# Fused decayed linear attention and dense layer: other order of the first loads, of the first groups' steps and of the third group's transposes

## The chip, the cores and the metric

The kernel runs on one core of one Trainium2 chip. The metric is the device time of one execution in microseconds (us). A core has five engines that work beside each other, each with a queue of its own in program order: TensorE (PE, matrix products; PEld is its loading of weights), VectorE (DVE), ScalarE (ACT), GpSimd (POOL) and SyncE (SP). POOL issues all loads that turn float32 into float16, SP issues the outputs and the transposes that the DMA engines make.

## The reference

Two parts in a row. First an attention without softmax, with a decay per head, worked block by block with a running state; then a dense layer with the Mish activation, `h * tanh(softplus(h))`.

```python
# q, k, v: (4, 8, 768, 64); lam: (8,)
for b in range(nb):                       # blocks of the sequence
    intra = einsum('bhic,bhjc->bhij', qb, kb) * Dmask      # lam ** (i - j) for i >= j
    intra = einsum('bhij,bhjd->bhid', intra, vb)
    inter = einsum('bhid,bhde->bhie', qb * lam_pow, kv_state)
    out[:, :, sl] = intra + inter
    kv_state = lam_block * kv_state + einsum('bhsd,bhse->bhde', kb * rev_pow, vb)
# dense layer: x (3072, 512), w_in (512, 2048), w_out (2048, 512)
h = x @ w_in
g = h * tanh(log1p(exp(h)))
return g @ w_out
```

## The kernel before

**Groups and chunks.** The sequence of 768 is cut into six groups `n` = 0 to 5 of 128 positions; each has four chunks `b` = 0 to 3, one for each of the four batches, of 128 positions and 8 heads. Chunks come in two pairs: 0 and 1 (lower), 2 and 3 (upper). A chunk's attention is: *turn* (k and q transposed, `turn_pe` on PE or `turn_dma` by DMA for a pair), *scores* (`raw_scores`: kT times qT), *masks* (`masked`, DVE, two products with the decay table `dm` to `sb`), `kd` (`decay_k`: k times its decay), *state* (product of `kd` and v, then `raw` and the new state `w`), *outputs* (`outputs`: q times state plus `sb` times v in PSUM bank z, then DVE makes `xn`). `xn` is turned to `xt` by PE (`back`) or by a DMA transpose. Group 0 has no state yet and goes through `first_outputs`.

**Dense layer.** A *unit* (`unit`, token `u`) is 128 of the 2048 hidden columns for the 512 rows of a group: four matmuls of 512 columns from `xt` and a quarter of w_in (`win[0]` to `win[3]`, four units each), then Mish on ACT into `hsg`. `two_units` does two of them for half the rows; `unit_part` does a piece of columns of a unit. Groups 4 and 5 use a seven-product scheme (`set_step`, tokens `m1` to `m7`). The second layer is `dense2_plain` (group 0, tokens `plain`) and `dense2` (groups 1 to 4, tokens `h`, with seven products), and `dense2_alone` for group 5 at the end.

**What sets the order.** Everything is written out by hand: `run(d, order, banks)` takes a string of tokens, and each token issues the instructions of one step on all its engines at that place. `s:0@0` is the scores of chunk 0 of group 0; without `@` an attention step belongs to the group after `d`. Each engine works through its own instructions in just this order. Semaphores hold back what is not ready. `fill:m` issues `m` products of zeros on PE (bank H). `k:b` puts `kd` on DVE, `k:b/p` on POOL; `st:b/tag/v` or `/p` puts the last product of the state on DVE or POOL. `load:k/1@2` is the load of k's upper pair of group 2, at POOL's turn. In the order of names below `win_71` to `win_74` are `win[0]` to `win[3]`, and `wout_75` to `wout_78` the four quarters of w_out; `vz` is v of group 0 with zeros between its heads.

**The start.** k and q of chunk 0 come as float32 through SP and ACT (`whole`) and are turned to float16 by ACT (`k0`) and DVE (`q0`). All other loads go through POOL, in the order in which they are written. The decay tables `dm` are made by DVE (`d:0`, `d:1`, four instructions each) and ACT (`e:0`, `e:1`, exponentials). `mish` loads ACT's table for the Mish function.

**Buffers.** k, q and v of later groups have four pair buffers each, so the load of a pair waits until the steps of an earlier pair that read its buffer are done.

Of the kernel before, what the change touches and what calls it, by code (L numbers as in the profile page):

```python
# [20 lines left out]
def kernel(  # L21
# [10 lines left out]
    nc = tc.nc  # L32
# [32 lines left out]

    def bank(tag, shape, dtype=F32):
        return ps.tile([128] + shape, dtype, name=f"b{tag}", tag=f"b{tag}")
# [49 lines left out]
    def load_wout(s):  # L117
# [13 lines left out]

    load_first("k", 0, queue=nc.sync)
# [5 lines left out]
    load_first("q", 1)  # L138
    load_first("v", 0, 2)
    load_first("k", 2, 2)  # L140
    nc.gpsimd.iota(ek, pattern=[[0, 1]], base=MID, channel_multiplier=-1,
                   allow_small_or_imprecise_dtypes=True)
    nc.gpsimd.iota(eq, pattern=[[0, 1]], base=-MID, channel_multiplier=1,
                   allow_small_or_imprecise_dtypes=True)
# [12 lines left out]

# [16 lines left out]
    def busy(m):  # L174

        t = bank("H", [4 * C])
        for _ in range(m):
            nc.tensor.matmul(t, kzero, kzero2, start=True, stop=True)

    def fill(m):  # L180

        t = bank("H", [C])
        for _ in range(m):
            nc.tensor.matmul(t, kzero, kzero, start=True, stop=True)
# [59 lines left out]
    def turn_pe(n, b, banks):  # L244
# [6 lines left out]
        for src, name, to, tag in zip(srcs, ("kT", "qT"), (kT, qT), banks):  # L251
            pt = bank(tag, [JP, C], F16)
# [27 lines left out]
    def raw_scores(n, b, tags):  # L280
        p_ = [bank(t, [JP, C]) for t in tags]
# [18 lines left out]
    def first_outputs(b, tag):  # L300
        po = bank(tag, [JP, C])
# [9 lines left out]
    def outputs(n, b, turn=None):  # L311

        done.add(("o", n, b))
        po = bank("z", [H, D])
        for j in range(JP):
# [15 lines left out]
        def later():  # L331
            pt = bank(turn, [JP, C], F16)
# [8 lines left out]
    def state(n, b, tag, eng, later=False):  # L341
        need("o" if n else "lbm", n, b if n else 0)
        done.add(("st", n, b))
        pv = bank(tag, [JP, 128])
# [24 lines left out]
    open_ = {}  # L369

    def unit_part(n, ni, tag, lo, hi, opens):
        need("x", n, range(lo // C, hi // C))
        if (n, ni) not in open_:
            open_[n, ni] = bank(tag, [GT])
        for kc in range(NKC):
# [5 lines left out]
    def unit_end(n, ni):  # L381
        nc.scalar.activation(h_tile(n)[:, ni, :], open_.pop((n, ni)), AF.Mish)  # L382
        done.update(have("g", n, ni, range(2)))

    def unit(n, ni, tag):
        unit_part(n, ni, tag, 0, GT, True)
# [9 lines left out]
    def two_units(n, ni, r):  # L396

        t = bank(next_bank(), [2, HC])
        cs = slice(r * HC, r * HC + HC)
# [79 lines left out]
    def set_step(o, step):  # L479
# [4 lines left out]
        if step == "m1":  # L484
            o.a = bank(o.banks[0], [2, HC])
            seven(o, 1, o.a, True)
        elif step == "seed":
            o.b = bank(o.banks[1], [2, HC])
            nc.scalar.activation(o.b, o.a, AF.Copy)
# [3 lines left out]
        elif step == "m5":  # L493
            o.c = bank(o.banks[2], [2, HC])
            seven(o, 5, o.c, True)
# [114 lines left out]
    def dense2(n):  # L610
# [3 lines left out]
        def half(p, blk):  # L614
            if blk == 0 and p in (1, 5, 3):
                m.g = bank("G", [2, HN])
            t = m.g if p in (1, 2, 5, 3) else m.h
# [3 lines left out]
            if p == 1:  # L621
                m.h = bank("H", [2, HN])
                nc.scalar.activation(m.h, m.g, AF.Copy)
# [24 lines left out]
    def dense2_plain(n, b, part, tag):  # L648

        if part == 0:  # L650
            open_[n, "out"] = bank(tag, [DMO])
        need("wout", part)
        po = open_[n, "out"]
        for kk in range(NKI // WS):
# [3 lines left out]
                             start=(ki == 0), stop=(ki == NKI - 1))  # L658
        if part == WS - 1:
# [58 lines left out]
    def run(d, order, banks=""):  # L718

        sets = [set_of(d, int(b[0]), b[1:]) for b in banks.split()]  # L720
        for token in order.split():
# [9 lines left out]
            elif op == "part":  # L731
                lo, hi = int(tags[1][0]) * C, int(tags[1][1]) * C
                unit_part(d, int(arg), tags[0], lo, hi, lo == 0)
# [136 lines left out]
```

## Time and profile before

| what | value |
|---|---|
| time, median of 3 runs | 204.89 us (204.76 to 205.01) |
| the profiled execution: time, span | 205.89 us, 204.1 us |
| mean granted clock of TensorE | 1.000 |
| busy: PE, PEld, DVE, ACT, POOL | 196.3, 147.1, 144.7, 96.1, 71.4 us |
| loads by POOL's queue | 13.37 MB |
| by the queues of SP and ACT | 12.26 MB and 0.33 MB |

The span runs from the first to the last instruction of the core; some 1.8 us of the time lie around it. An engine's busy time is the time in which at least one of its instructions runs. A row of the timeline has the start in us, the duration, the engine, the line, the operation and its tiles (output, then inputs), and in brackets the idle time before it and what ended that. PE's matmuls overlap, so the step from one start to the next tells more than the durations. A landing time runs from the start of the issuing instruction to the last byte.

### The profile page before, as it was taken

To read this page: it belongs to the slowest core of one execution; us is meant where nothing else is said; L and a number is where in the kernel's file an instruction comes from. 1 tells how busy PE (TensorE), PEld (TensorE's weight loads), DVE (VectorE), ACT (ScalarE), POOL (GpSimd) and SP (SyncE) were. 2 spreads that over 40 slices of the span, in tenths; PEclk is the share of its full clock that TensorE was granted. 3 is DMA by queue.
4 is the path that set the end of the run, shared out by engine and by line. 5 is a ranking of instruction groups with operands and counts; after the bars stand their busy time and mean duration, and the time that the engine had idled before them with its cause. 6 is when DMAs were issued, how large, how long until landed. Compare 5 with 4: busy or idle time off the path is not lost.

```text
span 204.1 us, 4535 instructions
## 1 busy us (share of the span) xinstructions
PE 196.3 (96%) x1879; PEld 147.1 (72%) x1879; DVE 144.7 (71%) x241; ACT 96.1 (47%) x170; POOL 71.4 (35%) x68
## 2 busy tenths in 40 slices
PE   7897999799999999999999999999999999999993
PEld 3675556588875556677576766868888988888893
DVE  6638558867784999379699795986949795097333
ACT  4554676757641124331534444145673474864310
POOL 7987454533254395047113377070000000000020
PEclk9999999999999999999999999999999999999999
DMA  8999999999969999999999399999210621002223
GB/s 128 130 166 206 165 181 157 172 206 190 139 128 115 206 171 177 126 182 151 115 203 162 79 80 130 127 285 130 79 29 22 115 71 55 2 0 72 85 76 129
DMA packets 109302, 26.24 MB, mean 129 GB/s; under 512 B 99426, under 2 KB 108770, under 8 KB 109282
## 3 DMA queue, kind: packets, MB, share of 16 engines
q0 software_dynamic: 77536, 13.37, 93.1%
q1 hardware_dynamic: 30560, 12.26, 31.7%
q10 hardware_dynamic: 1186, 0.33, 0.7%
q8 instruction: 14, 0.23, 0.5%
q14 instruction: 6, 0.05, 0.1%
HBM read 27.26 MB, written 6.29 MB: 164 GB/s over the span
## 4 chain that ended last, share of the span: by engine, by line
PE 89%; ACT 3%; DMA 3%; POOL 1%; DVE 1%; issue 1%; POOLq 0%
PE bG L604 15%; PE bH L604 13%; PE bA L376 7%; PE bB L376 7%; PE bC L376 6%; PE bB L471 3%; DMA vz<-in_v_dram 3%; PE bC L471 3%; PE bA L471 3%; PE bB L404 3%; PE bz L316 2%; PE bz L321 2%; PE bA L404 2%; PE bC L404 2%; PE be L285 2%; PE bA L657 2%
## 5 line engine op out<-in xcount | busy, mean ns | idle before, releaser
L356 POOL TENSOR_TENSOR w<-raw,lbm 128x512 f16<-128x512 f32 x14 | 21.1, 1509 | 54.9 <-DVE raw L354 54.9
L604 PEld LDWEIGHTS <-gsum 128*128 128x128 f16 x336 | 31.1, 98 | 4.6
L376 PEld LDWEIGHTS <-win 128*128 128x128 f16 x200 | 18.3, 98 | 16.3 <-issue 1.0
L604 PEld LDWEIGHTS <-hsg 128*128 128x128 f16 x240 | 23.2, 98 | 4.2
L324 DVE TENSOR_TENSOR xn<-bz,lq 128x512 f16<-128x512 f32 x20 | 13.8, 688 | 11.7 <-PE bz L321 11.6
L688 POOL TENSOR_TENSOR c<-p,u 128x512 f32<-128x512 f32 x1 | 1.3, 1260 | 58.3 <-DVE p L687 58.3
L604 PE MATMUL bH<-tsum,gsum 128*128 128x256 f16 x160 | 20.3, 273 | 0.0
L604 PE MATMUL bG<-wout,hsg 128*128 128x256 f16 x160 | 20.1, 273 | 0.0
L376 PE MATMUL bA<-xt,win 128*128 128x512 f16 (+2 forms) x72 | 17.6, 367 | 0.6 <-ACT xt L308 0.6
L295 DVE TENSOR_TENSOR sb<-be,dm 128x512 f16<-128x512 f32 x17 | 11.6, 684 | 8.4 <-PE bo L285 8.4
L278 DVE TENSOR_TENSOR kd<-kn,lk 128x512 f16<-128x512 f16 x20 | 16.6, 848 | 0.0
L376 PE MATMUL bB<-xt,win 128*128 128x512 f16 (+2 forms) x68 | 16.6, 367 | 0.0
L376 PE MATMUL bC<-xt,win 128*128 128x512 f16 x60 | 15.4, 379 | 0.0
L382 ACT ACTIVATE hsg<-bB 128x512 f16<-128x512 f32 x16 | 9.6, 598 | 12.1 <-PE bB L376 12.1
L382 ACT ACTIVATE hsg<-bA 128x512 f16<-128x512 f32 x17 | 10.2, 597 | 9.5 <-PE bA L376 9.5
L382 ACT ACTIVATE hsg<-bC 128x512 f16<-128x512 f32 x15 | 9.0, 599 | 10.1 <-PE bC L376 10.0
L471 PEld LDWEIGHTS <-wsum 128*128 128x128 f16 x128 | 12.5, 98 | 1.5
L559 DVE TENSOR_TENSOR gsum<-hsg 128x1024 f16<-128x1024 f16 x20 | 13.5, 680 | 0.0
L404 PEld LDWEIGHTS <-win 128*128 128x128 f16 x128 | 12.1, 98 | 1.8
L104 POOL DMA_DIRECT2D kn<-in_k_dram x10 | 11.8, 1179 | 2.9 <-PE bo L346 1.4
L104 POOL DMA_DIRECT2D vn<-in_v_dram x10 | 11.7, 1173 | 2.8 <-DMA win<-in_moe_w_in_dram 2.0
L104 POOL DMA_DIRECT2D qn<-in_q_dram x10 | 11.6, 1156 | 2.2 <-PE bA L376 0.9
(164 smaller groups left out, 406.0 us busy)
## 6 DMA issues: line engine op xcount, KB each, us to landing
out_dram<-osum SPq DMA_DIRECT2D x23, 256.0 KB, 2.4
kn<-in_k_dram POOLq DMA_DIRECT2D x11, 256.0 KB, 10.7
qn<-in_q_dram POOLq DMA_DIRECT2D x11, 256.0 KB, 12.7
vn<-in_v_dram POOLq DMA_DIRECT2D x10, 256.0 KB, 10.2
wout<-in_moe_w_out_dram POOLq DMA_DIRECT2D x4, 512.0 KB, 15.1
win<-in_moe_w_in_dram POOLq DMA_DIRECT2D x3, 512.0 KB, 12.2
vz<-in_v_dram POOLq DMA_DIRECT2D x2, 256.0 KB, 7.1
k<-in_k_dram SPq DMA_DIRECT2D x1, 256.0 KB, 3.3
```

The source lines that it names most:

```text
L104: nc.gpsimd.dma_start(out=tile_, in_=rows(src, n, 2 * bp, 2))
L278: eng.tensor_tensor(out=kd[n, b], in0=kn[n, b], in1=bc(lk, 2, D), op=ALU.mult)
L285: nc.tensor.matmul(p_[t][:, j, :], kT[n, b][rs, j, :], qT[n, b][rs, j, :], start=True, stop=True)
L295: nc.vector.tensor_tensor(out=sb[n, b, t], in0=p_[t], in1=dm[:, t], op=ALU.mult)
L324: nc.vector.tensor_tensor(out=xn, in0=po, in1=bc(lq, 2, D), op=ALU.mult)
L356: decay = lambda: eng.tensor_tensor(out=w_new, in0=raw, in1=lbm, op=ALU.mult)
L376: nc.tensor.matmul(open_[n, ni][:, lo:hi], win[ni // 4][:, kc, (ni % 4) * 128 : (ni % 4) * 128 + 128], xt[n][:, kc, lo:hi], start=(opens a ...
L382: nc.scalar.activation(h_tile(n)[:, ni, :], open_.pop((n, ni)), AF.Mish)
L404: nc.tensor.matmul(t[:, u, :], win[ni // 4][:, kc, m : m + 128], xt[n][:, kc, cs], start=(u == 0 and kc == 0), stop=(kc == NKC - 1), skip_ ...
L471: nc.tensor.matmul(t[:, u, :], lhs, rhs, start=(fresh and u == 0 and kk == 0), stop=(kk == 1), skip_group_check=True)
L559: nc.vector.tensor_tensor(out=gsum[n, i][:, ks, :], in0=a, in1=b, op=op)
L604: nc.tensor.matmul(t, lhs(kk, blk), rhs(kk)[:, lo:hi], start=(fresh and kk == 0), stop=(kk == HK - 1), skip_group_check=True)
```

## The change

- **First loads.** q and k of the upper pair of group 0, and its v, come as single chunks. The upper half of `win[0]` (columns 256 to 512) is loaded right behind the second chunk's k, its lower half far later and in one piece instead of two. `ek` and `eq` (`iotas`) are made later. v of group 1's lower pair comes behind `win[3]`.
- **Order of steps.** All six groups' token strings are reordered; the first three most. In group 0, `q0` stands ahead of the decay tables on DVE, the exponentials behind the first turn on ACT, and `mish` behind the third output. The first whole unit is 10 and not 2. Zero products: 64 in smaller pieces instead of 38.
- **kd on POOL.** Seven of the `kd` products move from DVE to POOL (`k:3/p@1`, `k:1/p`, `k:2/p`, `k:3/p` while group 1's units run, and `k:0/p`, `k:1/p`, `k:3/p` later).
- **Third group.** Loads of k for a pair need that the turn of the same pair two groups earlier was issued; `turn` and `load` tokens stand further apart.
- **Helpers.** `unit_part` and `dense2_plain` may take their parts in any order (the first one opens the bank); `pieces` and `parts` only keep account of banks and parts while the kernel is written out, and issue nothing.

POOL's queue from its first load on (`kn`, `qn`: k and q; 128x8x64 is one chunk, 128x16x64 a pair; `win_71` at 128x4x128 is a quarter of `win[0]`). Before:

```order
L94 DMA kn<-in_k_dram 128x8x64
L136 ISA
L136 IOTA rel 128x128
L94 DMA qn<-in_q_dram 128x8x64
L94 DMA vz_69<-in_v_dram 128x16x64
L94 DMA kn<-in_k_dram 128x16x64
L141 IOTA ek 128x1
L143 IOTA eq 128x1
L94 DMA qn<-in_q_dram 128x16x64
L94 DMA vz_70<-in_v_dram 128x16x64
L113 DMA win_71<-in_moe_w_in_dram 128x4x128 x2
L113 DMA win_71<-in_moe_w_in_dram 128x4x256
```

With the change, from the iota on:

```order
L146 IOTA rel 128x128
L117 DMA win_71<-in_moe_w_in_dram 128x4x256
L96 DMA qn<-in_q_dram 128x8x64
L96 DMA vz_69<-in_v_dram 128x16x64
L96 DMA qn<-in_q_dram 128x8x64
L96 DMA kn<-in_k_dram 128x8x64 x2
L96 DMA vz_70<-in_v_dram 128x8x64
L96 DMA qn<-in_q_dram 128x8x64
L137 IOTA ek 128x1
L139 IOTA eq 128x1
L117 DMA win_71<-in_moe_w_in_dram 128x4x256
L96 DMA vz_70<-in_v_dram 128x8x64
```

Half of `win[0]` moved ahead of the second chunk's q; the upper pair's q, k, k, v, q stand singly behind the first v, and the last v behind the other half of `win[0]`.

PE where the last pieces of units 0 and 1 end and the first whole unit starts. Before (`win_71` is `win[0]`, so unit 2):

```order
L376 MATMUL bB<-xt,win_71 128x128
L376 LDWEIGHTS win_71
L376 MATMUL bB<-xt,win_71 128x128
L376 LDWEIGHTS win_71
L376 MATMUL bC<-xt,win_71 128x512
```

With the change (`win_73` is `win[2]`, so unit 10):

```order
L394 MATMUL bB<-xt,win_71 128x128
L394 LDWEIGHTS win_71
L394 MATMUL bB<-xt,win_71 128x128
L394 LDWEIGHTS win_73
L394 MATMUL bC<-xt,win_73 128x512
```

The first unit reads another quarter of w_in, whose load stands two places further on in POOL's queue.

ACT around the turn of chunk 2 of group 1, while group 0's last units run (`hsg` are Mish activations, `xt<-bG` the copy of a turned-back output, `kT<-bH` and `qT<-bz` the copies of a turn). Before:

```order
L382 ACTIVATE hsg<-bB 128x512
L336 ACTIVATE xt<-bG 128x4x128
L260 ACTIVATE kT<-bH 128x512
L260 ACTIVATE qT<-bz 128x512
L382 ACTIVATE hsg<-bC 128x512
L336 ACTIVATE xt<-bG 128x4x128
```

With the change:

```order
L401 ACTIVATE hsg<-bB 128x512
L269 ACTIVATE kT<-bH 128x512
L269 ACTIVATE qT<-bz 128x512
L349 ACTIVATE xt<-bG 128x4x128
L401 ACTIVATE hsg<-bC 128x512
L401 ACTIVATE hsg<-bA 128x512
L349 ACTIVATE xt<-bG 128x4x128
```

The copies of the turn stand ahead of the copy of the first output, which came first.

The diff, cut (of each table of tokens the beginning):

```diff
@@ load_pair
             for i in (2 * bp, 2 * bp + 1):
                 need({"k": "kd", "q": "turn", "v": "o"}[t], n - 2, i)
+                if t == "k":
+                    need("turn", n - 2, i)
...
@@ first loads
     load_first("k", 1)
     nc.gpsimd.iota(rel, pattern=[[1, C]], base=0, channel_multiplier=-1,
                    allow_small_or_imprecise_dtypes=True)
-    load_first("q", 1)
-    load_first("v", 0, 2)
-    load_first("k", 2, 2)
...
-    load_first("q", 2, 2)
-    load_first("v", 2, 2)
-    load_win(0, 0, 128)
-    load_win(0, 128, 256)
-    load_win(0, 256, WQ)
-    load_win(2)
-    load_win(1)
-    for t in "kqv":
-        load_pair(t, 1, 0)
-    load_win(3)
-    for t in "kqv":
-        load_pair(t, 1, 1)
+    def run_loads(order):
+        for token in order.split():
+            t, *args = token.split("/")
+            args = [int(x) for x in args]
...
+    run_loads("""
+        w/0/256/512 q0/1 v0/0/2 q0/2 k0/2 k0/3 v0/2 q0/3 iotas w/0/0/256 v0/3 w/2 w/1 k/1/0 q/1/0
+        w/3 v/1/0 k/1/1 q/1/1 v/1/1""")
@@ group 0's attention
-        k0 d:0 q0 e:0 d:1 fill:6 pe:0/Gz@0 e:1 fill:6 s:0@0 mask pe:1/Gz@0 heads fill:4 first:0/C
...
+        k0 q0 fill:4 d:0 d:1 fill:3 pe:0/Gz@0 fill:3 fill:5 s:0@0 e:1 fill:3 fill:4 e:0 pe:1/Gz@0
+        fill:3 fill:7 s:1/AB@0 mask heads first:0/C mask fill:1 fill:3 pe:2/Gz@0 first:1/C s:2@0
...
@@ group 0's units
-        u:2 u:3 st:0/e/v@0 k:2@0 u:8 st:1/o/v@0 k:3@0 load:k/0@2 load:q/0@2 load:v/0@2 wout:0
...
+        u:10 wout:0 u:9 load:q/1@2 load:k/0@2 u:11 u:2 st:0/e/v@0 k:2@0 st:1/o/v@0 load:q/0@2
...
@@ unit_part
-        if (n, ni) not in open_:
+        opens = (n, ni) not in open_
+        if opens:
             open_[n, ni] = bank(tag, [GT])
@@ dense2_plain
-                             start=(ki == 0), stop=(ki == NKI - 1))
-        if part == WS - 1:
+                             start=(not made and kk == 0), stop=(kk == NKI // WS - 1),
+                             skip_group_check=True)
+        made.append(part)
+        if len(made) == WS:
```

More of the change, by code (lines that the diff above doesn't have):

```diff
@@ L64, in need @@
         assert not missing, missing
+    pieces = set()
     def bank(tag, shape, dtype=F32):
@@ L182, in fill @@
         t = bank("H", [C])
+        pieces.add("H")
         for _ in range(m):
@@ L331, in later @@
         def later():
+            pieces.add(turn)
             pt = bank(turn, [JP, C], F16)
@@ L381, in unit_end @@
     def unit_end(n, ni):
+        need("part", n, ni, range(4))
         nc.scalar.activation(h_tile(n)[:, ni, :], open_.pop((n, ni)), AF.Mish)
@@ L488, in set_step @@
             o.b = bank(o.banks[1], [2, HC])
+            assert o.banks[1] not in pieces
             nc.scalar.activation(o.b, o.a, AF.Copy)
@@ L622, in half @@
                 m.h = bank("H", [2, HN])
+                assert "H" not in pieces
                 nc.scalar.activation(m.h, m.g, AF.Copy)
@@ L648, in dense2_plain @@
     def dense2_plain(n, b, part, tag):
-        if part == 0:
-            open_[n, "out"] = bank(tag, [DMO])
+        if (n, b) not in parts:
+            parts[n, b] = (bank(tag, [DMO]), [])
+            pieces.discard(tag)
+        po, made = parts[n, b]
         need("wout", part)
-        po = open_[n, "out"]
         for kk in range(NKI // WS):
@@ L802 @@
+        fill:4 mask pe:3/Gz@0 fill:1 fill:1 k:1@0 fill:8 first:2/C s:3@0 states mish fill:6
+        part:0/A/03 fill:2 mask fill:2 fill:1 first:3/C k:0@0 fill:1 fill:2 part:1/B/03
+        part:0/A/34 part:1/B/34 end:0 end:1""")
     run(0, """
-        u:2 u:3 st:0/e/v@0 k:2@0 u:8 st:1/o/v@0 k:3@0 load:k/0@2 load:q/0@2 load:v/0@2 wout:0
-        wout:1 wout:2 wout:3 load:k/1@2 load:q/1@2 load:v/1@2 u:9 st:2/e/v@0 u:10 st:3/o/v@0 masks
-        u:11 u:4 u:5 pe:0/Hz k:0 u:6 u:7 s:0 mask pe:1/Hz k:1 u:12 o:0 st:0/H/v/l s:1 mask decay:0
@@ L806 @@
-        u:13 back:0 pe:2/Hz k:2 u:14 o:1 st:1/H/v/l s:2 mask decay:1 back:1 pe:3/Hz u:15""")
+        u:10 wout:0 u:9 load:q/1@2 load:k/0@2 u:11 u:2 st:0/e/v@0 k:2@0 st:1/o/v@0 load:q/0@2
+        k:3@0 k:1 u:5 u:3 masks u:7 pe:0/Hz u:6 wout:2 st:3/o/v@0 st:2/e/v@0 wout:3 pe:1/Hz
+        load:v/0@2 u:13 s:0 k:0 wout:1 mask u:12 u:8 load:k/1@2 o:0 u:4 s:1 pe:2/Hz back:0 u:14
+        mask st:0/H/v/l o:1 u:15 st:1/H/v/l back:1 s:2 load:v/1@2 pe:3/Hz decay:1 k:2 decay:0 mask""")
     run(1, """
-        k:3@1 two:0/0 two:2/0 o:2@1 st:2/H/p@1 s:3@1 mask two:4/0 two:6/0 back:2@1 o:3@1
@@ L815 @@
-        busy:1 h h""")
+        two:4/0 two:2/0 two:6/0 o:2@1 k:3/p@1 load:k/0@3 s:3@1 two:0/0 two:8/0 mask back:2@1 o:3@1
+        k:1/p two:10/0 st:3/H/v@1 back:3@1 two:12/0 pe:0/Hz two:4/1 turn:1 two:0/1 st:2/H/p@1
+        two:14/0 s:0 mask pe:1/HG k:0 two:6/1 two:14/1 o:0 st:0/H/v s:1 two:2/1 plain:0/1 two:10/1
+        mask o:1 q:0/0 q:0/1 st:1/H/p load:v/0@3 two:12/1 load:q/0@3 q:1/01 k:2/p plain:0/0
+        two:8/1 plain:1/1 plain:1/2 plain:2/1 s:2 mask plain:1/0 plain:0/2 s:3 o:2 turn:0@3 mask
```

77 lines of the change are left out of this document (47 added, 30 removed).

## The prediction

> **What bounds the kernel now.** I read the page's busy line first, then the stretches, the waits of PE and the timeline.
>
> ```profile
> PE 196.3 (96%) x1879; PEld 147.1 (72%) x1879; DVE 144.7 (71%) x241; ACT 96.1 (47%) x170; POOL 71.4 (35%) x68
> ```
> ```profile
> 0.00:20.70 20.70, 17.24 (x159) 12.33 (x160) 12.65 (x31) 10.84 (x20) 17.33 (x24) 1.00 1.60 158
> ...
> 32.00:40.00 8.00, 6.87 (x86) 4.45 (x85) 7.15 (x12) 4.97 (x11) 3.62 (x4) 1.00 2.42 162
> 40.00:190.00 150.00, 150.00 (x1442) 114.47 (x1441) 114.44 (x180) 70.16 (x124) 43.13 (x34) 1.00 1.18 123
> 190.00:204.10 14.10, 10.87 (x116) 9.76 (x113) 4.10 (x10) 1.79 (x3) 1.26 (x1) 1.00 0.27 93
> ```
>
> In the stretches (length, then PE, PEld, DVE, ACT and POOL busy, granted clock, DMA share, GB/s) PE never stops between 40 and 190 us. Nothing that the change does to loads, transposes or DVE there can gain; it can only cost. The last stretch (3.23 us idle) runs the same final part. What can be gained lies in two places: the start, up to the first whole unit of the dense layer, and 8.00 - 6.87 = 1.13 us of idle PE between 32 and 40.
>
> ```profile
> 20.70 1.03 PE L376 MATMUL bC<-xt,win 128*128 128x512 f16 x4
> 21.56 1.03 PE L376 MATMUL bA<-xt,win 128*128 128x512 f16 x4
> ...
> 22.65 1.03 PE L376 MATMUL bB<-xt,win 128*128 128x512 f16 x4
> ```
> ```profile
> PE bz L316 <- ACT qT L260: 0.6, 1, 0.6
> ...
> PE bG L334 <- DVE xn L324: 0.2, 1, 0.2
> PE bH L254 <- DVE raw L354: 0.2, 1, 0.2
> ```
>
> Up to 20.70 PE has made the first group's attention and units 0 and 1; there unit 2 starts (a unit is four matmuls, 0.86 from start to start), at 22.65 unit 8, the first on w_in's third quarter. The changed order has the same work ahead of that point, and then unit 10. So the first term is when that point comes; zero products ahead of it count as busy, but are no work.
>
> **The first stretch.** What the loads can give:
>
> ```profile
> 6.00:7.00 1.00, 0.90 (x9) 0.90 (x10) 1.00 (x5) 0.74 (x2) 1.00 (x3) 1.00 0.96 61
> ...
> 9.00:10.00 1.00, 0.48 (x6) 0.22 (x5) 0.70 (x2) 0.65 (x4) 1.00 (x3) 1.00 2.41 154
> 16.00:17.00 1.00, 0.50 (x12) 0.32 (x8) 0.49 (x1) 0.62 (x2) 1.00 (x2) 1.00 1.34 207
> ```
> ```profile
> 3.50 1.15 POOL L94 DMA_DIRECT2D vz<-in_v_dram  x1
> ...
> 5.94 1.19 POOL L94 DMA_DIRECT2D qn<-in_q_dram  x1
> ...
> 8.25 3.73 POOL L113 DMA_DIRECT2D win<-in_moe_w_in_dram  x5
> ```
> ```profile
> vz<-in_v_dram POOLq DMA_DIRECT2D x1, 256.0 KB, 6.4
> ```
> ```profile
> qn<-in_q_dram POOLq DMA_DIRECT2D x1, 256.0 KB, 7.3
> ```
> ```profile
> win<-in_moe_w_in_dram POOLq DMA_DIRECT2D x1, 512.0 KB, 10.4
> ```
>
> q, k and v pass at 154 KB/us, w_in at 207, and between 6 and 7 the engines ran nearly dry (61): the first v had been issued at 3.50 and its data was not yet there. It landed at 9.9. The change puts 256 KB of w_in (1.24 us) into that hole. POOL's issues move by one w_in issue (3.73 / 5 = 0.75), so v of the first pair moves by 0.75: I take its landing at 10.65. Behind it come five single chunks of 128 KB, 128/154 = 0.83 each: q2 11.5, k2 12.3, k3 13.1, v2 14.0, q3 14.8; then w_in's lower half 16.0, v3 16.9. In all, ahead of the end of w2 (the third quarter, units 8 to 11) the same bytes pass as before, less the hole. Before, w2 was the fourth of the five w_in issues (about 10.5) and landed at 10.5 + 10.4 = 20.9; with 0.5 to 0.7 us of the hole filled: 20.2 to 20.4. The other end: if the time from issue counted, not the bytes ahead, w2 (issued at about 12.25, behind more issues) would land at 22.65. Adding 512/207 to v3's 16.9 would even give 19.4. I take 20.3, since the queue is busy from 7 us on and the bytes ahead of w2 decide, and keep both far ends.
>
> The Trainium skill (page "DMA: Bandwidth & Descriptors", section "Anatomy of one DMA — SWDGE (gpsimd) path") gives each such DMA a fixed cost of about 2.0 us beside its bytes, and speaks against splitting loads. By it three more DMAs would be an estimated 6 us, 210 in the end, if the fixed part were not hidden. The rows differ: from 9 to 10 the data moves at 154 KB/us without a gap while q of the upper pair, issued at 5.94, takes 7.3 to land, with k and v in flight beside it: the fixed part overlaps.
>
> Now the engines, with the durations of these rows:
>
> ```profile
> 3.62 1.01 DVE L201 SCALAR_TENSOR_TENSOR dm<-rel,lnb,gone 128x128 f32<-128x128 f32 x4
> ...
> 4.66 0.63 ACT L793 ACTIVATE dm<-dm 128x512 f32<-128x512 f32 x1
> ...
> 5.36 0.68 DVE L795 CAST qn<-q 128x512 f16<-128x512 f32 x1 [0.73 <-DMA q<-in_q_dram]
> ...
> 8.08 0.69 DVE L295 TENSOR_TENSOR sb<-be,dm 128x512 f16<-128x512 f32 x1 [1.00 <-PE bo L285]
> ...
> 11.53 1.03 PE L184 MATMUL bH<-kzero 128*128 128x128 f16 x8
> ...
> 13.64 1.28 ACT L790 ACT_TABLE_LOAD   x1
> ...
> 15.56 0.61 PE L184 MATMUL bH<-kzero 128*128 128x128 f16 x8
> ```
>
> DVE now casts q first, and so stands until 5.36; the two decay tables follow at 6.04 to 8.1 (2 x 1.01) instead of one at 3.62, their exponentials on ACT at 8.15 to 9.4. The first two masks therefore run at about 10.1 to 11.4, against 8.08 before. The first output (which before waited for v at 9.9) starts at 11.4, with v there since 10.65: a late table costs 0.75 beyond the load. From there each step hangs on the one before: masks of chunk 1 to 12.7; turns of chunk 2 (k2 at 12.3) at 12.85; its scores 14.35, masks to 16.05; third output 16.4; its copy on ACT 17.1 to 17.7. The table load (1.28) now stands behind that copy and not ahead of the second one: 17.7 to 19.0. DVE puts one kd and the lbm copies ahead of the last masks, which end at 18.65. Fourth output 18.8, its copy 19.3 to 19.9; the remaining pieces of units 0 and 1 end at 20.55. That is 0.15 ahead of 20.70. The 26 further zero products (64 against 38) lie in these waits: at 0.08 to 0.13 each (0.61 / 8, 1.03 / 8) 2 to 3 us of PE that would be idle. If the waits around them shrank, those right ahead of the pieces (11, 0.9 us) would cost. Term one: -0.15, with ends of -0.7 (tables not late, since DVE's order alone sets that) and +1.95 (w2 at 22.65).
>
> **32 to 40 us.**
>
> ```profile
> 18.22 1.17 POOL L104 DMA_DIRECT2D qn<-in_q_dram  x1
> ```
> ```profile
> qn<-in_q_dram POOLq DMA_DIRECT2D x1, 256.0 KB, 16.4
> ```
> ```profile
> 35.09 0.39 PE L254 MATMUL bz<-ident,qn 128*128 128x128 f16 x4
> ...
> 35.34 0.59 ACT L336 ACTIVATE xt<-bG 128x512 f16<-128x512 f16 x1
> ...
> 36.29 0.62 ACT L260 ACTIVATE qT<-bz 128x512 f16<-128x512 f16 x1
> ...
> 36.96 0.38 PE L316 MATMUL bz<-w,qT 128*128 128x128 f16 x4 [0.62 <-ACT qT L260]
> ```
>
> The turn of chunk 2 ends on PE at 35.31 (its last four transposes, of 128 columns each, take a quarter of a unit's 0.86); the outputs of chunk 1 need bank z, which ACT empties (qT) only at 36.9, because the copy of xt ran first (0.59). Between them stood one unit (0.86). Now the turn-back (0.23), the unit and a state product (0.23) stand between, 1.32, and ACT copies kT and qT ahead of xt: z is free some 1.1 after the turn. The 0.62 goes. The second turn-back waited 0.23 for xn: 0.57 of PE work (a state product, one scores) stood between, now a unit and a state product, 1.1: gone. The wait for raw (0.19) keeps its distance (scores and turn-back change places) and stays. What is late next is q of the upper pair of group 1, which landed at 18.22 + 16.4 = 34.6 and, with the hole filled, would at 34.2, while its turn now stands at 20.55 + 13.4 = 33.95 by the durations of the steps between: a wait of 0.2. w3 lands at about 29.2 for unit 13 at 29.35. Term two: -0.62 - 0.23 + 0.2 = -0.65, with ends of -0.85 (q in time) and -0.2 (q at 34.6).
>
> **From 40 us on.** Seven kd products move from DVE to POOL.
>
> ```profile
> 40.61 0.68 DVE L278 TENSOR_TENSOR kd<-kn,lk 128x512 f16<-128x512 f16 x1
> ...
> 46.95 2.36 DVE L278 TENSOR_TENSOR kd<-kn,lk 128x512 f16<-128x512 f16 x2
> ...
> 47.12 1.65 POOL L356 TENSOR_TENSOR w<-raw,lbm 128x512 f16<-128x512 f32 x1 [1.81 <-DVE raw L354]
> ```
>
> The Trainium skill (page "GPSIMD Engine Reference", section "Engine selection") calls two-input work there about 2 times slower and says that it shares interfaces with VectorE. The rows agree: DVE's two kd took 2.36 while POOL's 1.65 ran, against 2 x 0.68 alone. So DVE gains nothing for sure, 7 x 0.68 less against up to 7 x 1.0 more; with 35.6 of 150 us idle it covers both. POOL's own queue: kd stands behind loads that wait for earlier loads, but each kd is used 4 us or more later. Without that cover one late kd would cost PE a microsecond.
>
> Group 3's transposes, a k load that ran alone (issued at 59.92), and the landing of the first transpose:
>
> ```profile
> kn<-in_k_dram POOLq DMA_DIRECT2D x1, 256.0 KB, 4.7
> ```
> ```profile
> kT<-kn SPq DMA_TRANSPOSE x1, 9.3
> ```
> ```profile
> 80.03 4.09 SPq L268 DMA_TRANSPOSE qT<-qn  x1
> ```
>
> Beside queued loads one issue took 4.09 and one landing 9.3, and PE was full all the same. Holding POOL's loads back shortens these, which is worth 0. But group 4's k load of the lower pair now stands on POOL behind the state product of group 3's chunk 1: near 89, where its scores stand at about 107 (both by adding the durations of the steps). Load 4.7, one issue 4.09 and a landing of 9.3 make 18.1 of these 18 us if the transposes still collide; well under that if not. Without that cover PE stands at the scores, and what lies on SP behind the transposes (x of chunks 2 and 3, outputs) is late with them. Term three: 0, ends 0 and +1.0.
>
> Sum: -0.15 - 0.65 + 0 = -0.8. The profiled execution took 205.89 (span 204.10), 1.0 over the median 204.89; a difference carries over: 204.1.
>
> **Rivals.** (1) The waits move and do not go: the queue does not use the hole, q of group 1's upper pair lands at 34.6, and PE waits 0.65 there in place of the 0.85 removed. -0.15 - 0.85 + 0.65 gives 204.5. For it: these loads wait behind the same bytes. Against: 61 KB/us at 6 to 7. (2) Slower: unit 10, the first whole unit, needs w2 2 us sooner than before (unit 2 needed only the upper part of the first quarter; w2 was first used at 22.65). At w2 = 22.65 the start is 1.95 late, less 0.85 in 32 to 40 (the q wait vanishes): 206.0. It decides from a landing of about 21.55 on. For it: five more issues of 0.75 to 1.15 stand ahead. Against: bytes, not issues, set the landings after 8 us. (3) The page's fixed cost per DMA, exposed: 210; the rows speak against it. (4) Tables and masks overlap better and the start gains 0.7, no q wait: -0.7 - 0.85, 203.3.
>
> **Numbers.** About 0.2% (0.41 us) is what a measurement can tell from no change. Forecast 0.48; (4) 0.07; (1) 0.25, within 0.2%; (2) 0.17; (3) 0.03. So faster 0.55, same 0.25, slower 0.20. The range goes from (4)'s 203.3, rounded down to 203.2, to 205.6, which takes in part of (2).
>
> **What the changed profile would show.** Right: DMA above 130 GB/s between 6 and 7 us; v at about 10.7; the first unit on the third w_in quarter at 20.2 to 20.9 with no wait for its load; the PE waits for qT and xn in 30 to 40 gone; PE full from 40 to 190. Wrong: PE waiting for w_in ahead of unit 10 or unit 13, for q of group 1, or any idle PE after 40, above all at scores whose transposes are late.

## The result, and the profile after

The change made the kernel slower: 207.31 us (median of 4 runs, 206.94 to 208.69) against 204.95 (204.76 to 205.16) for the kernel before on the same chip, ratio 1.0127 with a 95% interval of 1.008 to 1.0174. The profiled execution took 206.94 (span 205.2). Ratios here and below leave out executions more than 1.5% slower than the fastest of their kernel, and they are not the quotient of the two medians beside them.

The stretches of the changed kernel, cut as for before (length, then PE, PEld, DVE, ACT and POOL busy, granted clock, DMA share, GB/s):

```profile
0.00:20.64 20.64, 17.47 (x185) 11.89 (x186) 13.53 (x31) 10.89 (x20) 19.08 (x27) 1.00 1.61 162
...
32.00:40.00 8.00, 7.79 (x98) 5.52 (x97) 5.63 (x10) 5.84 (x12) 4.24 (x5) 1.00 2.12 173
40.00:190.00 150.00, 147.97 (x1421) 112.31 (x1419) 109.21 (x177) 68.83 (x122) 42.93 (x36) 1.00 1.08 122
190.00:205.20 15.20, 11.90 (x125) 10.69 (x123) 4.98 (x11) 2.25 (x4) 1.26 (x1) 0.99 0.26 87
```

The 1.13 us of idle PE between 32 and 40 are down to 0.21. But the long middle, where PE never stopped before, now has 2.03 us of idle time. PE's waits between 40 and 192 us (total, times, longest) name all of it; for before this view is empty:

```profile
PE bC L491 <- DVE xsum L466: 1.0, 1, 1.0
PE be L360 <- DVE sb L305: 0.5, 1, 0.5
PE bB L491 <- DVE bC L523: 0.5, 1, 0.5
```

That these three were the loss, and what makes them, took experiments, and so did a second thing: the one profile of before from which I predicted was itself 0.94 us above the median of the other runs. A second profile of the same kernel (204.77, span 203.0) gives the better scale. Some rows of its timeline:

```profile
9.42 0.62 PE L306 MATMUL bC<-sb,vz 128*128 128x128 f16 x8 [1.06 <-DMA vz<-in_v_dram]
10.36 0.62 PE L184 MATMUL bH<-kzero 128*128 128x128 f16 x8
11.32 0.40 PE L254 MATMUL bG<-ident,kn 128*128 128x128 f16 x4 [0.34 <-DMA kn<-in_k_dram]
12.74 0.40 PE L254 MATMUL bz<-ident,qn 128*128 128x128 f16 x4 [1.03 <-DMA qn<-in_q_dram]
...
19.61 1.03 PE L376 MATMUL bC<-xt,win 128*128 128x512 f16 x4
```

The first whole unit starts at 19.61, not 20.70, and every later step stands 1.09 earlier. That is made of two pieces. The first is a load: the wait for q of the upper pair, issued at 5.94 and 5.95, ends 0.53 later in the first profile than here (12.74):

```profile
13.27 0.61 PE L254 MATMUL bz<-ident,qn 128*128 128x128 f16 x4 [0.28 <-DMA qn<-in_q_dram]
```

The second is TensorE's rate. The first profile had 1.03 us for eight zero products at 11.53; here the same eight take 0.62, and from start to start it is 107 ns against 56. The scores of chunk 2, which follow the turn of that q without a wait, start at 14.77 and at 13.69, which is the other 0.55. TensorE was slow up to about 14 us in the one execution and at full rate from about 5.5 us in the other, while the granted clock reads 1.00 in both. The changed kernel at the same places:

```profile
11.01 0.55 PE L317 MATMUL bC<-sb,vz 128*128 128x128 f16 x7 [0.22 <-DVE sb L305]
12.35 0.40 PE L263 MATMUL bG<-ident,kn 128*128 128x128 f16 x4 [0.35 <-DMA kn<-in_k_dram]
...
20.64 1.03 PE L394 MATMUL bC<-xt,win 128*128 128x512 f16 x4
```

So against the second profile the start is 1.03 later. Neither start is fixed: in other profiles below the old one stands at 19.55 to 19.89 (three) and the changed one at 20.06 to 20.84 (eight). The whole sum, by where the same work stands on PE:

| us | before, first profile | before, second | changed | changed against the second, step by step |
|---|---|---|---|---|
| first whole unit starts | 20.70 | 19.61 | 20.64 | +1.03 |
| first `two` of group 0 starts | 40.26 | 39.17 | 38.80 | -1.40 |
| `m1` of group 4 starts | 137.77 | 136.68 | 137.15 | +0.84, of it 0.51 the stop near 99 |
| last matmul ends | 200.86 | 199.78 | 201.90 | +1.65, of it 1.04 and 0.48 the stops at 139 and 143 |

The sum is +2.12. Of it 0.46 (0.33 and 0.13) is no wait that the profile shows.

### The profile page after: what moved, and what is told of

It is laid out like the page before. It is cut to its first block, busy times and chain, and to the rows that moved or that the text cites. A ratio compares the mean times of both kernels' runs of the same rounds, so it can differ in the third digit from the quotient of the medians.

```text
span 205.2 us, 4581 instructions
## 1 busy us (share of the span) xinstructions
PE 196.5 (96%) x1905; PEld 146.5 (71%) x1905; DVE 140.8 (69%) x238; ACT 96.4 (47%) x170; POOL 72.9 (36%) x73
## 4 chain that ended last, share of the span: by engine, by line
PE 81%; DMA 6%; DVE 6%; POOL 4%; issue 1%; ACT 0%; POOLq 0%; DVEq 0%
PE bG L627 13%; PE bH L627 12%; PE bA L394 6%; PE bB L394 5%; PE bC L394 5%; PE bB L491 3%; DMA xt<-xn 3%; DMA qn<-in_q_dram 3%; PE bC L491 3%; PE bB L424 3%; PE bz L333 2%; PE bA L491 2%; PE bA L424 2%; PE bC L424 2%; PE bz L328 2%; PE bA L683 2%
## 5 line engine op out<-in xcount | busy, mean ns | idle before, releaser
L370 POOL TENSOR_TENSOR w<-raw,lbm 128x512 f16<-128x512 f32 x10 | 13.8, 1384 | 51.2 <-DVE raw L368 51.2
L627 PE MATMUL bH<-tsum,gsum 128*128 128x256 f16 x160 | 20.3, 273 | 0.0
L305 DVE TENSOR_TENSOR sb<-bo,dm 128x512 f16<-128x512 f32 x17 | 11.6, 681 | 0.0
```

The costliest lines, as they stand in the source:

```text
L305: nc.vector.tensor_tensor(out=sb[n, b, t], in0=p_[t], in1=dm[:, t], op=ALU.mult)
L370: decay = lambda: eng.tensor_tensor(out=w_new, in0=raw, in1=lbm, op=ALU.mult)
L627: nc.tensor.matmul(t, lhs(kk, blk), rhs(kk)[:, lo:hi], start=(fresh and kk == 0), stop=(kk == HK - 1), skip_group_check=True)
```

## The experiments

Each run is given with its median against that of before on the same chip, and the ratio with its 95% interval. The text strings are the tokens of `run`.

**Which part loses.** First, the changed loads, the first group and the sixteen units, with the strings of `run(1)` to `run(5)` as before; then the reverse.

> The changed first loads and the changed order of the first group and of the dense layer's sixteen units (up to 40 us); from the second string of group 1 on everything stands as before. Theory (later groups lose it): the first part alone gains what the traces show at 40 us, 1.46 us, so 203.5 (ratio 0.993), and PE does not stop between 45 and 190. Rival (the first part brings the loss, by loads that arrive otherwise): 206 to 207.3, and PE stops after 40 us although the later order is the old one.

205.24 against 205.11, ratio 1.0005 (0.9991 to 1.002). The first part alone neither gains nor loses. In its profile it is 0.2 ahead of the second profile of before near 40 us (the first `two` starts at 38.97, against 39.17), and then the seam to the old strings costs 0.39 (PE waits for masks at 41.66).

> The reverse: first loads, first group and the sixteen units as before, the changed order from 40 us on with its seven kd products on POOL. Theory (later groups lose): 204.95 plus the 2.0 us of new idle PE time, and up to 1.8 more if the medians count, so 207.0 to 208.8. Rival (the first part brings the loss): 204.5 to 205.3.

208.61 against 205.11, ratio 1.0165 (1.0137 to 1.0193): the loss lies in the later strings. PE's waits in its profile, an execution of 211.05, are the same three and a fourth:

```profile
PE bC L491 <- DVE xsum L466: 2.4, 1, 2.4
PE bA L394 <- DMA xt<-xn: 1.6, 1, 1.6
PE be L360 <- DVE sb L305: 0.5, 1, 0.5
PE bB L491 <- DVE bC L523: 0.5, 1, 0.5
```

**Is it the order of groups 4 and 5, or kd on POOL?** One run has the strings of `run(4)` and `run(5)` as before, one has `k:b` for all seven `k:b/p`.

> The changed kernel with the last two strings (groups 4 and 5) as before. Theory (the stops at 139 and 143 us, 1.04 and 0.48, come from the changed order of group 4, whose first outputs stand closer to the fifth product of its dense layer): both go, the stop near 99 us (0.5) stays: 207.3 - 1.5 = 205.8. Rival (they come from the load of v of group 5's upper pair, which still stands at the end of group 3's string, right ahead of the x transposes): they stay in part, 206.5 to 207.3.

207.76 against 205.11, ratio 1.0142 (1.0103 to 1.018). The wait for the sums stays and is 1.41 here. So the order of groups 4 and 5 does not make it, and the place that the rival named, the end of the string of `run(3)`, is left. The stop of 0.48 at 143 is gone in this profile, so that one does need the changed order of group 4.

> The changed kernel with all seven kd products back on DVE, order unchanged. Theory: the stop near 99 us was DVE's queue with a kd stretched to 2.33 beside POOL; kd of 0.7 there and seven more elsewhere nearly even out: 206.8 to 207.8. Rival (products on POOL are what costs, by slowing DVE and holding the loads back): 205 to 206, and the stops at 99 and 140 us go.

208.48 against 205.11, ratio 1.0165 (1.0147 to 1.0183): not the cause, for the loss is no smaller. Whether kd on POOL is a help stays open, since the interval overlaps that of the changed kernel. With all kd on DVE one of them is late:

```profile
70.36 0.40 PE L360 MATMUL bH<-vn,kd 128*128 128x128 f16 x4 [1.46 <-DVE kd L287]
```

**The same kernel again.**

> The kernel before once more, for its profile: the profiled execution of before took 205.89, 0.94 over the median of its other runs. If the start differs from execution to execution (loads that land late), unit 2 starts up to 1 us ahead of 20.70 here, or the 1.13 us of idle PE between 32 and 40 are smaller, and all from 40 us on stands in the same distances. If the difference lies behind 190 us, the start is at 20.70 again.

204.77. This is the second profile above: the difference lies at the start, all of it, and half of it (0.53) in loads that landed late, as supposed.

**The stop at 139: a load beside the transposes.** The timeline of the changed kernel there (SPq is SP's queue of DMA issues):

```profile
131.10 3.61 SPq L339 DMA_TRANSPOSE xt<-xn  x2
...
131.75 1.27 POOL L370 TENSOR_TENSOR w<-raw,lbm 128x512 f16<-128x512 f32 x1 [4.16 <-DVE raw L368]
132.96 1.20 POOL L108 DMA_DIRECT2D vn<-in_v_dram  x1
...
136.64 0.69 DVE L370 TENSOR_TENSOR w<-raw,lbm 128x512 f16<-128x512 f32 x1
...
139.76 0.43 DVE L466 TENSOR_TENSOR xsum<-xt 128x512 f16<-128x512 f16 x1 [1.83 <-DMA xt<-xn]
...
140.24 0.60 PE L491 MATMUL bC<-xsum,wsum 128*128 128x256 f16 x4 [1.04 <-DVE xsum L466]
```

The second transpose of `xt` can go out when its `xn` is there (132.79 + 0.69 = 133.48), and its data comes at 139.7, 6.2 us later. DVE stands idle for it for 1.83 and PE for 1.04. (By its tokens the `w` here is that of group 4's chunk 3; the expectations name it after `run(3)`, in which group 3's units run.) Half a microsecond ahead of that transpose, POOL issued the load of v for group 5. First attempt, the token moved on in the text:

```diff
-        ... st:3/e/v h u:14 u:15 load:v/1@5"""
+        ... st:3/e/v h u:14 u:15"""
-        g:2 m1:0 seed:0 x:0123 g:01 h turn:1 m2:0 m5:0 m6:0 S:0/A
+        g:2 m1:0 seed:0 x:0123 g:01 h turn:1 m2:0 m5:0 m6:0 load:v/1@5 S:0/A
```

> The changed kernel with one load moved: v of group 5's upper pair, issued on POOL about 5 us later, behind the sixth product of group 4's first set and not right ahead of the last transposes of group 3's x. Theory (the load takes the DMA engines from the transposes, whose data comes late for the sums): the transposes land about 4 us after their issue and not 6, the stops at 139 (1.04) and 143 us (0.48) go: 207.3 - 1.5 = 205.8, and the runs scatter by less than before. Rival (the sums are late by DVE's own queue): 207.3, the stop stays.

208.35 against 205.26, ratio 1.0132 (1.0096 to 1.0168). This told nothing, because the load did not move: POOL has no work between the two places, and issued it 1.21 behind `w` as before, beside the transposes:

```profile
133.22 1.27 POOL L370 TENSOR_TENSOR w<-raw,lbm 128x512 f16<-128x512 f32 x1 [4.89 <-DVE raw L368]
134.43 1.21 POOL L108 DMA_DIRECT2D vn<-in_v_dram  x1
```

What holds a load back is the work ahead of it on its queue. In before that was a second `w`, and the load went out 3.9 behind the last x transpose:

```profile
133.03 1.19 SPq L327 DMA_TRANSPOSE xt<-xn  x1
...
133.69 1.26 POOL L356 TENSOR_TENSOR w<-raw,lbm 128x512 f16<-128x512 f32 x1 [7.62 <-DVE raw L354]
135.35 1.65 POOL L356 TENSOR_TENSOR w<-raw,lbm 128x512 f16<-128x512 f32 x1 [0.40 <-DVE raw L354]
136.94 1.21 POOL L104 DMA_DIRECT2D vn<-in_v_dram  x1
```

The change had moved the second `w` to DVE. So one token was undone:

```diff
-        ... G:01 G:23 h st:3/e/v h u:14 u:15 load:v/1@5"""
+        ... G:01 G:23 h st:3/e/p h u:14 u:15 load:v/1@5"""
```

> The changed kernel with one token undone: the last product w of group 3 (st:3) back on POOL, ahead of the load of v of group 5's upper pair. In the run with that load later in the text it went out at the same place in POOL's queue (1.21 us behind the w of st:2, while the second x transpose was on its way), since POOL has nothing in between; here POOL must wait for raw (136.6) and the load is issued near 137.9 instead of 132.96. Theory (the load takes the DMA engines from the transposes): the transposes land about 3 us after their issue as in before, not 6.2, the stop at 139 us (1.04) goes and that at 143 (0.48) with it: 207.3 - 1.5 = 205.8. Rival (the transposes are late for another reason, and the order of DVE and of the outputs sets the stop): 207.0 to 207.5, with the stop as it was.

206.28 against 205.09, ratio 1.0045 (1.0016 to 1.0074), where the changed kernel has 1.0127. The timeline:

```profile
130.84 3.60 SPq L339 DMA_TRANSPOSE xt<-xn  x2
...
136.42 1.65 POOL L370 TENSOR_TENSOR w<-raw,lbm 128x512 f16<-128x512 f32 x1 [3.67 <-DVE raw L368]
136.90 1.45 DVE L466 TENSOR_TENSOR xsum<-xt 128x512 f16<-128x512 f16 x1
...
138.02 1.20 POOL L108 DMA_DIRECT2D vn<-in_v_dram  x1
```

The load is 5 us later, the sums start at 136.90 without a wait for the transposes, and both stops, at 139 and 143, are gone. The theory holds: some 1.7 us (0.8% of 205.09) of the loss hang on that token. Over all profiles of the changed order it is the same: where the load goes out 0.3 to 0.6 ahead of the second transpose, that takes 5.6 to 7.5 us to land (nine profiles), and where POOL's `w` holds the load back, 2.4 to 4.3 (six). The load is not all that slows transposes there, for the first of the two took 6.5 with it and still 5.4 without. Whether the token suffices was tried in before (`st:2/e/p` to `st:2/e/v` in `run(3)`):

> The kernel before with one token of the change: the last w of group 3 on DVE and not on POOL. The load of v behind it is then issued at 133.9 and not at 135.85, beside the x transpose issued at 133.3. Theory: that transpose lands up to 3 us later (139.5 for 136.4) and the fifth product of group 4 (138.57) waits for the sums: 0.5 to 2.0 slower, 205.6 to 207.1. Rival (before has room enough there, only the changed order's closer outputs made it bite): 205.1.

205.39 against 205.29, ratio 1.0007 (0.9981 to 1.0034): not by itself. The load went out at 134.79, right behind the first `w` there, but the last x transpose had been issued at 132.92, 1.9 ahead of it, and landed at 137.06; the sums at 137.16 had no wait. So both were needed, the early load and the changed order, which puts the last transpose behind it.

**The stop near 99: DVE full.** The timeline of the changed kernel:

```profile
91.76 2.33 DVE L287 TENSOR_TENSOR kd<-kn,lk 128x512 f16<-128x512 f16 x1
...
92.21 1.32 POOL L370 TENSOR_TENSOR w<-raw,lbm 128x512 f16<-128x512 f32 x1
...
95.81 0.68 DVE L582 TENSOR_TENSOR gsum<-hsg 128x1024 f16<-128x1024 f16 x1
96.52 0.69 DVE L582 TENSOR_TENSOR gsum<-gsum,hsg 128x1024 f16<-128x1024 f16 x1
...
98.33 0.68 DVE L305 TENSOR_TENSOR sb<-be,dm 128x512 f16<-128x512 f32 x1
...
99.06 0.40 PE L360 MATMUL be<-vn,kd 128*128 128x128 f16 x4 [0.51 <-DVE sb L305]
```

One kd takes 2.33 while POOL's `w` runs, two sums stand ahead of the masks, and the state product waits for the bank that a mask reads. The two sums were moved behind the masks (in `run(2)`), first with the edit that moved nothing, then with the token above:

```diff
-        ... k:2 mask h k:3 G:01 h o:2 u:6 h mask u:5 st:2/e/p
+        ... k:2 mask h k:3 h o:2 u:6 h mask G:01 u:5 st:2/e/p
```

> As the one before, and the sums of group 2's rows 0 and 1 (two DVE additions of 0.69) moved behind the last masks of group 4's chunk 3. Theory (the stop near 99 us, 0.51, is DVE's queue, full from 88 to 101 us): it goes too, 205.3. Rival (the stop comes from the kd of 2.33 stretched beside POOL): 0.51 is less than the 1.38 moved, so it would go as well; but then DVE has no idle time up to 101 and the sums stop the dense products behind them: 205.8 or more.

207.22 against 205.26, ratio 1.0086 (1.0047 to 1.0124), where the run without it had 1.0132.

> The same token undone, and the two sums of group 2 behind the last masks of group 4's chunk 3, which took the stop near 99 us away and 0.8 us in all. Theory: 207.3 - 1.5 - 0.8 = 205.0, as fast as before, since the start is still 0.8 to 1.0 later than in before and 20 to 40 us gives 1.4 back. Rival (stops move on and come out elsewhere behind 100 us): 206 or more.

205.41 against 205.09, ratio 1.0016 (0.9986 to 1.0046), against 1.0045 without it. In both pairs the intervals overlap, but the ratio falls in both, and the stop near 99 is gone in both. How much of that stop is the sums and how much the stretched kd these runs do not separate, since both accounts expected it to go. From `two` to `m1` the second kernel takes 97.51 us (38.94 to 136.45), just as before (97.51).

**The scatter: the same mechanism near 77.** In several profiles PE also stopped for the last transpose of group 2's `x`, in others not. One that stops is the run with three edits below:

```profile
72.99 1.22 SPq L339 DMA_TRANSPOSE xt<-xn  x1
...
73.01 1.21 POOL L108 DMA_DIRECT2D qn<-in_q_dram  x1
...
78.54 1.02 PE L394 MATMUL bA<-xt,win 128*128 128x512 f16 x4 [1.66 <-DMA xt<-xn]
```

The load of q goes out 0.02 us behind the transpose, again because a `w` (`st:2/H`) was moved from POOL to DVE. In the run with two mendings the same two stand 0.23 apart, and PE does not stop:

```profile
72.91 1.22 SPq L339 DMA_TRANSPOSE xt<-xn  x1
...
73.14 1.21 POOL L108 DMA_DIRECT2D qn<-in_q_dram  x1
```

This transpose lands at 75.94, that issued at 72.99 lands at 78.50. So it is over all twelve profiles with this order: where the load is issued between 0.09 ahead of the transpose and 0.16 behind it, the transpose takes 5.1 to 5.5 us and PE stops for 1.12 to 1.66 (four profiles); where it is issued 0.23 to 1.36 behind, 2.7 to 3.0, and PE does not stop (eight). A tenth or two of a microsecond between the two queues separates the cases, and so the stop comes and goes; that the transposes are merely issued late is ruled out by the pair above. The `w` was moved back, on top of the two mendings:

```diff
-        h plain:2/2 q:2/0 st:2/H/v load:q/1@3
+        h plain:2/2 q:2/0 st:2/H/p load:q/1@3
```

> As with both fixes (w of group 3's st:3 on POOL, two sums of group 2 later), and w of group 2's last state product (st:2/H) on POOL as in before, so that the four loads behind it are issued near 75.0 and not at 73.00, 0.3 behind the issue of group 2's last x transpose (72.67). Theory (the loads slow that transpose, and by luck more or less): it lands within 4 us, the stop near 77 us (1.1 to 1.7 in four of the profiles) does not come, and the runs scatter less: 204.5 to 204.9 with the slowest below 206, against 205.41 (204.06 to 206.91). Rival (the transposes are late because they are issued late): the scatter stays, 205.2 to 205.8.

204.60 against 205.29, ratio 0.9971 (0.9948 to 0.9994): faster than the changed kernel, and 0.3% faster than before by an interval that barely leaves out 1. Eleven of its 12 runs lie between 204.13 and 205.57; one took 208.74, and why stays open. The same place in its timeline:

```profile
72.78 1.23 SPq L339 DMA_TRANSPOSE xt<-xn  x1
...
73.71 1.65 POOL L370 TENSOR_TENSOR w<-raw,lbm 128x512 f16<-128x512 f32 x1 [0.46 <-DVE raw L368]
75.30 1.21 POOL L108 DMA_DIRECT2D qn<-in_q_dram  x1
```

The transpose has 2.5 us ahead of the load, and PE has no wait of 0.2 or more between 40 and 192 us.

**The start.** The first loads as before, all else changed; the quarter of w_in moved behind the single chunks (`w/0/256/512` behind `v0/3`); all three edits (`st:3/e/p`, `G:01` and this); the first group's string as before with the changed loads.

> The changed kernel with the first loads as before (pairs of chunks, w_in behind them). Theory (the single chunks and the early quarter of w_in are worth little by themselves): unit 10 starts 0.2 to 0.8 later than at 20.64 because the third quarter of w_in lands at 20.9, so 207.5 to 208.1. Rival (the single chunks cost issues and delay the start): 206.3 to 206.9.

211.55 against 205.26, ratio 1.0289 (1.0247 to 1.0331). The first unit starts at 22.25, 1.6 later and not 0.2 to 0.8, and from the first `two` to `m1` 1.8 more are lost, 1.45 of it in waits for masks near 44: the changed order needs the changed loads. How much of the 1.6 is the loads is not shown, because in this profile the granted clock reads 0.63, 0.50 and 0.50 in the three us from 13 to 16. The loss is not the clock's alone: two executions with a mean clock of 1.00 took 210.33 and 212.04.

> The changed kernel with the first load of w_in (upper half of the first quarter, 256 KB) moved behind the single chunks of q, k and v. Theory (the quarter ahead of v and k sets the start: the scores of chunk 2 wait for k until 12.35, against 11.32 in the second profile of before): k lands about 1 us earlier, the first whole unit starts at 19.7 to 20.0 and not at 20.64: 206.4 to 206.7. Rival (masks and tables on DVE set the start, the loads had room): 20.5, 207.2.

207.80 against 205.09, ratio 1.0131 (1.0094 to 1.0169): nothing. The first unit starts at 20.64 as in the changed kernel; PE now waits for masks (0.38 at 11.55, 0.38 at 18.77) where it waited for v, k and q. k of chunk 2 lands at 11.00, 1.3 earlier, so the first half of the theory holds and the second does not.

> All three edits together. Theory: the sums of the three, 205.0 - 0.8 = 204.2, ratio 0.995 to 0.998 to before: the gain of 1.4 us between 20 and 40 us is kept and the losses are gone. Rival (they share waits): 205 to 206.

205.84 against 205.09, ratio 1.0007 (0.9977 to 1.0036): as fast as before, no better than without the third edit. Its profile has the stop near 77 shown above.

> The changed kernel with the first group's string (tables, zero products, scores, masks, pieces of units 0 and 1) as before, and the changed loads. Theory (late tables and masks set the changed start, since moving the w_in quarter did nothing): the first whole unit starts at 19.6 to 20.0, 206.3 to 206.7. Rival (the loads set it too: k of chunk 2 lands at 12.35 against 11.32): 20.6 as now, 207.3.

209.87 against 205.29, ratio 1.0212 (1.0181 to 1.0244). The first unit starts at 20.91. But this run does not tell whether the old string alone would free the start, for TensorE's clock was lowered in it. PE waits for v until 10.33 and is busy for 0.62 of the two us before 10; it had been at full rate from about 7 us, and now the granted clock falls and eight zero products take 1.03 again:

```profile
9.00:10.00 1.00, 0.29 (x6) 0.11 (x3) 0.42 (x1) 0.01 (x1) 1.00 (x4) 1.00 2.43 155
...
12.00:13.00 1.00, 1.00 (x12) 1.00 (x11) 1.00 (x2) 0.00 (x0) 1.00 (x2) 0.50 2.43 155
```

The clock is back at 1.00 from 14 us. All five executions of this kernel have a mean clock of 0.992, so it is no accident of the profiled one. PE also stops for the transposes at both places (1.7 each).

Both undone together (the early quarter of w_in and the new first string), with the three mendings behind 70 us; then also with units 2 and 3 ahead of 10 and 9:

> The changed kernel with the three mendings behind 70 us (both w on POOL, two sums later), the first group's string as before and the w_in quarter behind the single chunks; single chunks and the order of the sixteen units stay changed. Theory (late data of v and k and late masks each hold the start at 20.6, so only both together free it): the pieces of units 0 and 1 end by 19.6 to 19.9; unit 10 then waits for the third quarter of w_in until about 20.3, so little is gained over 204.6: 204.2 to 204.6. Rival (TensorE's slow rate up to 14 us sets the start whenever it comes): 20.7 to 20.9, 204.6 to 205.

204.98 against 205.13, ratio 0.9965 (0.9936 to 0.9994), no gain over the run with three mendings. The first unit starts at 20.03, after a wait:

```profile
20.03 1.04 PE L394 MATMUL bC<-xt,win 128*128 128x512 f16 x4 [0.43 <-DMA win<-in_moe_w_in_dram]
```

The pieces end by 19.6, as the theory said, and unit 10 waits for w_in's third quarter. PE also stops for 0.51 at 107.25, for group 3's `xt`.

> The same, with units 2 and 3 ahead of 10 and 9, so that the first whole unit needs only the first quarter of w_in. Theory: it starts at 19.6 to 19.9 without a wait and keeps 0.5 to 0.9 of it: 203.7 to 204.1. Rival (w_in's later quarters are late by as much, or TensorE is slow): 204.5 or more.

204.98 against 205.13, ratio 0.9989 (0.9959 to 1.002). The first unit starts at 19.27 without a wait, but the first `two` is at 38.71: of the 1.57 gained on 20.84 only 0.29 are left against the 39.00 of the run with three mendings. One thing that takes it back is q of group 1's upper pair:

```profile
34.24 0.40 PE L263 MATMUL bz<-ident,qn 128*128 128x128 f16 x4 [0.84 <-DMA qn<-in_q_dram]
```

**Zero products.** Before with 12 more of them (`fill:8` ahead of `d:0`, `fill:10` for the second `fill:6`):

> The kernel before with 12 more zero products of 128 columns ahead of the first scores (8 ahead of the first turn, 4 ahead of the scores). Theory (its slower executions are those in which TensorE runs at two thirds of its rate up to 14 us, as in its first profile): more early work brings the full rate earlier and always, the matmuls of four transposes at 6 us take 0.40 in the profile, the median stays within 0.2 of 205.1 and the slowest runs (up to 206.9) come nearer to it. Rival (zero products only stand in the way): 0.5 to 1.0 slower, 205.6 to 206.1.

206.23 against 205.29, ratio 1.0041 (1.0014 to 1.0068). The time went the rival's way, but not for its reason: the first unit starts at 19.57, so the start lost nothing, and TensorE is quick at 6 us. Its profile stops for 1.17 us at 108 us, at the first unit behind group 3's transposes, as does that of before with `w` on DVE (0.98). The `xt` that it waits for took 4.1 us from issue to landing (104.27 to 108.36), against 2.7 in the second profile of before (104.31 to 107.03). Why is open, and also whether the other executions stop there, of which none took less than 205.80. The theory's premise falls too: apart from one execution of 336.56, the six longest of before beside these runs (206.84 to 207.31) have a mean granted clock of 0.983, and all others 0.992 or more, while the first profile reads 1.00.

## Why the prediction was wrong

**Term three, from 40 us on, is the step that failed.** It was put at 0, with 0 and +1.0 as ends. Measured are stops of 2.03 us (0.51, 1.04, 0.48), and 1.1 to 1.7 more near 77 us in some profiles of the changed order. "It can only cost" was right, and so was naming idle PE after 40 as what would show it wrong. Three of its reasonings fell:

- I counted the seven kd that left DVE for POOL, but not the four state products `w` that went the other way. Two of them are the tokens `st:3/e/v` and `st:2/H/v`, and with these POOL lost the work that had held the loads back. The prediction looked only at what is queued on POOL behind added work, not at what comes out earlier when work is taken off. Putting the one back was worth 1.7 us.
- "With 35.6 of 150 us idle it covers both" is the average of DVE. Between 91 and 99 us, ahead of the stop, DVE was busy for 7.86 of 8.00, and what decided was its order.
- Group 3's transposes, the transposes at which the change aims, I looked at for kT and qT, and named x only as what would be late behind them. The ones that came late are the `xt` of groups 2 and 4, which stand on the same queue. Where I did look, the reasoning held in this profile: k of group 4 was issued at 88.72 (forecast near 89), and no scores waited for a transpose. In the run that only moved a token in the text, scores did wait for qT, 0.68 at 126.28.

**Term two, 32 to 40 us: right in kind, too small.** The waits for qT and xn are gone, as forecast, and unit 13 did not wait for w3; that for q of group 1, taken as 0.2, did not come, since q landed at 33.80 (it does come when the start is earlier, 0.84 above: rival 1's mechanism). Measured from the first unit to the first `two`: -1.40, for a forecast of -0.65 with -0.85 as its end. What was mis-sized are the waits themselves. I took them from the idle time in the brackets; the steps from start to start show more. In the second profile five steps between the same 168 matmuls are too long: the outputs of chunks 0 and 1 behind qT (0.25 at 31.58, 0.58 at 35.87), the turn-back behind xn (0.30 at 37.27), and the turns of k and q (0.36 at 37.87, 0.19 at 34.19), 1.68 in all. With the change one is left, 0.28 at the turn of k. The difference is the 1.40.

**Term one, the start: -0.15 by the profile that I had, +1.03 by the second.** Point by point it was close: v landed at 10.52 (forecast 10.65), DMA ran at 152 GB/s between 6 and 7, and the first unit started at 20.64 (forecast 20.55) without a wait for w2. That landed at 19.46, by the sum of 19.4 that the prediction set aside, and not at 20.3 (so rival 2 fell). What failed is the sentence "a difference carries over": the execution I compared with had its loads 0.53 late and TensorE slow up to 14 us, which together made its start 1.09 late. In the other one the steps wait for v until 9.42 and for k until 11.32, and the 256 KB of w_in put ahead of them show: 12.35. Undoing both the early quarter and the new string gave 0.6 and 1.4. Undoing the quarter alone gave nothing, as the masks then held the start at the same place; the string alone was not tested at full clock. A row for eight matmuls of 1.03 at 11.53 beside one of 0.61 at 15.56 stood in the prediction; I used both as prices of zero products and did not ask why they differ.

**The other rivals.** The fixed cost of about 2.0 us per DMA did not show: single chunks landed 0.8 apart, and the changed order with the old pair loads stands at 1.0289 against 1.0127, slower and not faster. The count was off as well: nine of POOL's loads stand ahead of w2 before and eleven with the change, so it is two more, where the prediction has three in one place and five in another. Rival 4 fell by its start, which was 0.06 and not 0.7 ahead of 20.70.

The Trainium skill (page "TensorE: Matmul & The Clock Gate", section "Part 1: The HAM clock gate (the "warmup" mystery)") says that TensorE starts at half its clock, leaves it after about 3.4 us of sustained work, and that this point varies from execution to execution. The traces agree on the half (107 against 56 ns from start to start) and that the point varies (14 us in one profile, 5.5 in the other). But 14 us is far longer than the 3.4 us that the Trainium skill gives, although PE was busy for 0.85 or more of each us from 2 to 9, so here the measurement decides.

## What to carry to other kernels

An instruction taken off a queue lets everything behind it go earlier: when a product leaves the engine that issues loads, ask which transfer is then in flight beside the new load, and who waits for that one. Moving a load's place in the program moves nothing unless its queue has other work, or a wait, between the two places. Take two profiles of the kernel before ahead of adding up tenths of a microsecond, or look for equal instructions with unequal durations in one. And size a wait by the step from start to start, not by the idle time in the brackets: here that was 1.68 against 0.85.

## What the runs showed of the hardware that I had not expected

- One load of a pair (the 256 KB kind) issued 0.3 to 0.6 us ahead of a transpose by the DMA engines went with 5.6 to 7.5 us from that transpose's issue to its landing (nine profiles, near 133). With the load held back it was 2.4 to 4.3 (six).
- Near 77 the edge is sharp: with the load from 0.09 ahead to 0.16 behind the transpose, 5.1 to 5.5 us; from 0.23 to 1.36 behind it, 2.7 to 3.0.
- TensorE's low rate at the start (107 ns a step for 56) lasted to 14 us in one execution and to 5.5 in another of the same kernel, with a granted clock of 1.00 in both. In another kernel the same 107 ns came with a granted clock of 0.50 from 11 to 13 us, after TensorE had already been at full rate. So a granted clock of 1.00 did not rule out the low rate here.
- A `kd` on DVE took 2.33 instead of 0.68 beside one product of 1.32 on POOL: about as if it had waited for that product to end (93.53) and then run.
